# The order of all engine queues of a state-space convolution and feed-forward kernel, searched anew with altered planner costs

## Chip, cores and metric

One core of a Trainium2 chip. The metric is the time of one execution in microseconds, the median of several. The core's engines are TensorE (PE), VectorE (DVE), ScalarE (ACT), GpSimd (POOL) and SyncE (SP, which here issues DMAs); each runs its own queue of instructions in order and waits on semaphores.

## The reference

```python
x = A_q                                    # (1, 2048, 640), bf16
h = x + A_ref(layernorm(x), A_k, A_v, A_shift_k, A_ssm_k, A_ssm_D)
h2 = h + B_ref(layernorm(h), B_w_gate, B_w_up, B_w_down)

def A_ref(q, k, v, shift_k, ssm_k, ssm_D):
    k_shift = sum over t < 4 of k_pad[:, t:t + S, :] * shift_k[:, 3 - t]   # causal, per channel
    kv = k_shift * v
    y = irfft(rfft(kv padded to 2 S) * rfft(ssm_k padded to 2 S))[:S]       # causal long convolution, per channel
    return q * (y + kv * ssm_D)

def B_ref(x, w_gate, w_up, w_down):        # 640 -> 1728 -> 640
    return (silu(x @ w_gate) * (x @ w_up)) @ w_down
```

## The kernel before

The sequence is cut into four blocks of 512 rows. The long convolution is done block against block in a transformed domain: the four blocks of the filter are transposed and transformed (`ktrans`, `kfwd`, `kcomb`, tiles `KT`, `KO`, `C`, `R1`), each block of `kv` is formed (`kv`: short convolution on PE, transposed by DMA into `kvo`, times `v` on DVE) and transformed (`xfwd`: tiles `XH`, `FO`), products of block j of kv with block i - j of the filter are summed on DVE (`prod`, by far the most of DVE's work), and `inverse` gives rows again: DVE combines to `IE` and `IO`, PE multiplies with `itab`, ACT or DVE evicts, the gate with the normalized x and the second layer norm follow on ACT, DVE and POOL (which takes the power -1/2), and four DMA transposes put the block's normalized rows into `hnT`. `ffn` then does the up stage, thirteen PSUM tiles of ten matmuls (gate and up, 128 x 512 outputs) and one of five, each evicted twice by ACT (L964 with silu, L966) and multiplied on DVE (L968), and the down stage (L1000, L1012; for the last rows L983), added to x and stored. While PE does the feed-forward of block i, the other engines do the convolution of block i + 1.

The program is planned, not written in its final order. `g.add` records 921 tasks, numbered in order of recording, each with an engine, a planner's cost in nanoseconds and the data that it reads and writes. `ORDER` lists, for each engine, the numbers in the order in which its queue takes them. `schedule` walks the five queues with the costs, and from the modelled times it does two things only: it gives each PSUM tile one of four units (two banks each), the one that comes free first, and where PE would wait over 700 ns at the opening of a tile it puts `fill` idle matmuls of 192 columns (L250) before it. It also puts a wait behind a run of more than five independent DVE tasks. `emit` then writes the queues with their waits. `VECTOR` names the PSUM evictions that are done by DVE (L490 to L496) instead of ACT (L502).

What the numbers mean (block i's transform, say, is `xf` i):

| numbers | tasks |
|---|---|
| 0 to 4, 17 to 19, 57, 62, 67, 136 | first loads: identity, wcol, D row, ftab (3), itab (4), filter blocks (17, 57, 62, 67), kT of block 0 (18), v (19), x (136) |
| 13; 15, 16; 34 | warm-up matmuls; tables for the short convolution; adding D to the filter |
| 20 to 31 | kv of block 0: matmuls 20, 24, 28, evictions 21, 25, 29, PE transposes 22, 26, 30, products 23, 27, 31 |
| 32, 33, 35, 36; 58 to 61, 63 to 66, 68 to 71 | transposes of the filter (PE) and their evictions of 1280 columns |
| 37 to 56; 72 to 91; 94 to 113; 114 to 133 | filter transforms kf0 to kf3: PE task n, its eviction n + 1, then four DVE sums |
| 92, 93; 134, 135 | DVE combinations of filter blocks; the same by POOL's DMAs |
| 137 to 157; 327 to 342; 520 to 535; 727 to 741 | first layer norm of blocks 0 to 3 (338 a small DVE step of block 1, the last four each the normalized rows on ACT, L843) |
| 158 to 177; 343 to 362; 536 to 559; 750 to 769 | xf0 to xf3: PE task n, its eviction n + 1, then DVE sums |
| 182 to 221; 376 to 424; 583 to 631; 795 to 843 | inverse transform, gate and second layer norm: among them DVE's last combinations (188, 183; 383, 377, 384; 590, 591; 802, 796, 803), the powers on POOL (205, 212, ...), ACT steps ahead of them (204, 211, ...) and the hnT transposes (block 0: 200, 207, 214, 221; block 2: 604, 613, 622, 631; block 3: 816, 825, 834, 843) |
| 222 to 231 | loads of the feed-forward weights: GA, UA, GB, UB, PK, Wd |
| 232 on; 425 on; 632 on; 844 on | up stage of blocks 0 to 3: PE task n, gate eviction n + 1, up eviction n + 2, product n + 3 (the narrow tile has two of each) |
| 291 to 308; 484 to 501; 691 to 708; 903 to 919 | down stages, their evictions (487, 491, 496, 500 in block 1) and residual sums |
| 311, 504, 711; 312, 505, 712; 315 to 323, 508 to 516, 715 to 723 | loads of k and v of blocks 1 to 3, and the DMA transposes of the short convolution |

Of the kernel before, what the change touches and what calls it, by code (L numbers as in the profile page):

```python
# [58 lines left out]
class _Graph:  # L59
# [171 lines left out]
    def emit(self, block):  # L231
# [99 lines left out]
    """,  # L331
    "dve": """
# [10 lines left out]
    """,  # L343
    "pool": """
        8 10 6 11 5 9 7 151 202 216 195 205 209 219 198 212 134 336 135 403 421 394 412 529 610 619 628 601 736 822 813 840
        831
    """,
    "sp": """
# [4 lines left out]
}  # L353

VECTOR = """
    21 129
"""

def bass_sequential_preLN__ssm_conv_h3__swiglu_ffn__prompt_kernel(
# [38 lines left out]
    with ExitStack() as es:  # L398
# [54 lines left out]
        w = o + 16640  # L453
# [662 lines left out]
```

## Time and profile before

| | |
|---|---|
| runs | 268.63, 268.86, 268.97 us, median 268.86 |
| profiled execution | 268.22 us, of which the span is 266.3; granted TensorE clock 1.00 |
| PE | 254.0 us busy (95%), 1638 matmuls |
| DVE | 204.0 us (77%) |
| ACT | 203.9 us (77%) |
| POOL | 29.1 us (11%) |
| DMA | 28.47 MB moved in 43701 packets |
| matmuls of the up stages | 53.1 + 53.1 + 45.5 + 45.5 us by their modelled ends |

Busy times of PE overlap, since its matmuls are pipelined and their ends modelled (379 ns for one of 512 columns, where the next starts 0.22 us later). So idle time before an instruction tells more than busy time. Views that follow show instructions as start, duration, engine, line, operation, written and read tiles, with the idle time before it and its releaser in brackets.

### The profile page before, as it was taken

The page shows a single profiled execution, that of the slowest core. Times are in us where ns is not written, and L with a number is a line of the kernel's source. Part 1 is how long each engine was busy: PE and PEld are TensorE (multiplying, and loading weights), DVE is VectorE, ACT ScalarE, POOL GpSimd, SP SyncE. Part 2 cuts the span into 40 slices and gives each one's busy share as a digit, 9 for nine tenths or more (in the row PEclk, how much of TensorE's full clock was granted, in tenths as well). Part 3 has the DMA queues.
Part 4 walks back from the last instruction along what each step waited for, and adds up shares of the span by engine and source line. Part 5 has one row for each costly group of instructions (what it writes and reads, how often), then busy time and mean ns, then how long its engine had stood idle before and what let it go on. Part 6 is the DMA issues. An engine that isn't in the chain of part 4 may idle for free.

```text
span 266.3 us, 4177 instructions
## 1 busy us (share of the span) xinstructions
PE 254.0 (95%) x1638; PEld 142.1 (53%) x1638; DVE 204.0 (77%) x285; ACT 203.9 (77%) x392; POOL 29.1 (11%) x37
## 2 busy tenths in 40 slices
PE   7889888999999999999999999899999999999995
PEld 5567454545544646544445567444446674444563
DVE  0889999999999999999999999999895101330404
ACT  2689999999967999766979999678799982653600
POOL 0000314202030035000020041000300200000000
PEclk9999999999999999999999999999999999999999
DMA  6998919889966566331001734510000140000032
GB/s 155 335 333 266 342 57 227 131 194 315 178 111 108 81 173 105 55 117 81 4 0 19 184 79 93 146 78 1 2 0 0 22 79 0 0 2 0 0 127 74
DMA packets 43701, 28.47 MB, mean 107 GB/s; under 512 B 32289, under 2 KB 41378, under 8 KB 43682
## 3 DMA queue, kind: packets, MB, share of 16 engines
q1 hardware_dynamic: 41968, 25.58, 36.4%
q0 software_dynamic: 1056, 2.62, 5.7%
q8 instruction: 13, 0.21, 0.3%
q10 hardware_dynamic: 658, 0.01, 0.1%
q14 instruction: 6, 0.05, 0.1%
HBM read 15.69 MB, written 2.62 MB: 69 GB/s over the span
## 4 chain that ended last, share of the span: by engine, by line
PE 53%; ACT 23%; DVE 11%; DMA 6%; SPq 4%; issue 2%; POOL 0%; DVEq 0%
PE ps L941 16%; PE ps L942 15%; PE ps L1003 14%; SPq L514 3%; ACT xh L843 3%; ACT KT L502 3%; PE ps L610 2%; DMA kT<-in_A_k_dram 2%; ACT KO L502 2%; DMA ftab<-cst_ftab 2%; DMA hnT<-qo 2%; DVE gu L968 2%; PE ps L717 2%; ACT C L502 1%; ACT qo L884 1%
## 5 line engine op out<-in xcount | busy, mean ns | idle before, releaser
L1003 PE MATMUL ps<-Wd,gu 128*128 128x384 bf16 (+1 forms) x390 | 55.5, 299 | 0.1
L941 PE MATMUL ps<-hnT,GA 128*128 128x512 bf16 x140 | 53.1, 379 | 1.3 <-DMA hnT<-qo 1.1
L942 PE MATMUL ps<-hnT,UA 128*128 128x512 bf16 x140 | 53.1, 379 | 0.0
L1003 PEld LDWEIGHTS ps<-Wd,gu 128*128 128x128 bf16 x390 | 37.6, 98 | 17.1 <-issue 1.1
L941 PE MATMUL ps<-hnT,GB 128*128 128x512 bf16 x120 | 45.5, 379 | 0.0
L942 PE MATMUL ps<-hnT,UB 128*128 128x512 bf16 x120 | 45.5, 379 | 0.0
L966 ACT ACTIVATE ub<-ps 128x512 bf16<-128x512 f32 (+1 forms) x60 | 33.9, 567 | 14.9 <-PE ps L942 12.0
L964 ACT ACTIVATE gu<-ps 128x512 bf16<-128x512 f32 x52 | 30.4, 596 | 13.2 <-PE ps L942 13.1
L968 DVE TENSOR_TENSOR gu<-gu,ub 128x512 bf16<-128x512 bf16 x52 | 21.5, 421 | 23.8 <-ACT gu L964 15.8
L779 DVE TENSOR_TENSOR T<-X,C 128x2560 bf16<-128x2560 bf16 x20 | 29.7, 1486 | 0.2
L780 DVE TENSOR_TENSOR T<-X,C 128x2560 bf16<-128x2560 bf16 x20 | 29.7, 1486 | 0.1
L911 POOL TENSOR_TENSOR mv<-mv,half 128x1 f32<-128x1 f32 x16 | 16.1, 1010 | 69.1 <-ACT mv L904 69.1
L941 PEld LDWEIGHTS ps<-hnT,GA 128*128 128x128 bf16 x140 | 13.7, 98 | 18.4 <-DMA hnT<-qo 1.4
L610 PE MATMUL ps<-KT,ftab 128*128 128x320 bf16 x128 | 19.8, 300 | 3.5 <-ACT KT L502 1.1
L942 PEld LDWEIGHTS ps<-hnT,UA 128*128 128x128 bf16 x140 | 13.7, 98 | 15.6
L785 DVE TENSOR_TENSOR T<-T 128x1280 bf16<-128x1280 bf16 x24 | 19.5, 820 | 0.2
L941 PEld LDWEIGHTS ps<-hnT,GB 128*128 128x128 bf16 x120 | 11.7, 98 | 14.2 <-ACT gu L964 0.2
L942 PEld LDWEIGHTS ps<-hnT,UB 128*128 128x128 bf16 x120 | 11.8, 98 | 14.0
L831 POOL TENSOR_TENSOR st<-st,half 128x8 f32<-128x8 f32 x4 | 8.3, 2067 | 88.1 <-ACT st L825 88.1
L796 DVE TENSOR_TENSOR Y<-Y,T 128x2560 bf16<-128x2560 bf16 x12 | 17.8, 1484 | 0.0
L610 PEld LDWEIGHTS ps<-KT,ftab 128*128 128x128 bf16 x128 | 11.2, 98 | 10.9 <-ACT KT L502 2.0
L843 ACT ACTIVATE xh<-xh,st 128x640 bf16<-128x640 bf16 x16 | 14.7, 967 | 2.7 <-DVE st L833 2.7
(96 smaller groups left out, 381.9 us busy)
## 6 DMA issues: line engine op xcount, KB each, us to landing
kc<-in_A_ssm_k_dram SPq DMA_DIRECT2D x4, 640.0 KB, 9.4
xh<-in_A_q_dram SPq DMA_DIRECT2D x4, 640.0 KB, 4.1
vt<-in_A_v_dram SPq DMA_DIRECT2D x4, 640.0 KB, 4.5
out_dram<-xh SPq DMA_DIRECT2D x15, 160.0 KB, 1.9
Wd<-in_B_w_down_dram SPq DMA_DIRECT2D x1, 1280.0 KB, 6.3
C<-C POOLq DMA_DIRECT2D x1, 1280.0 KB, 9.6
C<-R POOLq DMA_DIRECT2D x1, 1280.0 KB, 9.4
UA<-in_B_w_up_dram SPq DMA_DIRECT2D x1, 1120.0 KB, 9.1
```

The lines of the kernel that those rows point to most:

```text
L610: last = e.matmul(pt.f(c, W), ftab[:, cs, j, f * P:(f + 1) * P], src[:, j, c * W:(c + 1) * W], start=(j == par), stop=(j == par + 2))
L779: g.add("dve", nm, lambda e, x=x, k=k, t1=t1: e.tensor_tensor(out=t1, in0=x, in1=k, op=ALU.mult), cdve(2560), r=[x, k], w=[t1])
L780: g.add("dve", nm, lambda e, x=x, k=ksw, t2=t2: e.tensor_tensor(out=t2, in0=x, in1=k, op=ALU.mult), cdve(2560), r=[x, k], w=[t2])
L785: g.add("dve", nm, lambda e, p=p, q=q, d=d, op=op: e.tensor_tensor(out=d, in0=p, in1=q, op=op), cdve(1280), r=[p, q], w=[d])
L796: g.add("dve", nm, lambda e, y=y, z=z: e.tensor_tensor(out=y, in0=y, in1=z, op=ALU.add), cdve(2560), r=[y, z], w=[y])
L843: g.add("act", nm, lambda e, j=j, xj=xj: e.activation(out=xj, in_=xj, func=ACTF.Identity, scale=s[:, 4, j:j + 1], bias=s[:, 5, j:j + 1]), ...
L941: e.matmul(pt.f(0, N), wg[:, c, f0:f0 + P], hnT[:, c, :], start=(c == 0), stop=(c == NC5 - 1))
L942: last = e.matmul(pt.f(1, N), wu[:, c, f0:f0 + P], hnT[:, c, :], start=(c == 0), stop=(c == NC5 - 1))
L964: g.add("act", nm, lambda e, pt=pt, gv=gv, a=ps_g, ts=ts: e.activation(out=gv, in_=pt.f(a[0], N, a[1])[:, ts], func=ACTF.Silu, scale=gain) ...
L966: g.add("act", nm, lambda e, pt=pt, uv=uv, a=ps_u, ts=ts: e.activation(out=uv, in_=pt.f(a[0], N, a[1])[:, ts], func=ACTF.Copy, scale=gain) ...
L968: g.add("dve", nm, lambda e, uv=uv, gv=gv: e.tensor_tensor(out=gv, in0=gv, in1=uv, op=ALU.mult), cdve(n), r=[gv, uv], w=[gv])
L1003: last = e.matmul(pt.flat(c1 - c0, P + c0), slots[fb][:, j * P:(j + 1) * P], Wd[:, fb, c0:c1], start=(fb == 0 and not second), stop=(fb == ...
```

## The change

Every queue's order is replaced, most tasks moving by a few places. `VECTOR` gives eviction 33 to DVE in place of 21, which goes to ACT. Four kinds of cost are altered: an ACT step that takes scale and bias per row from 186 to 219 ns above its base, the small ACT steps of the layer norms from 160 to 185, the evictions of the up stage at least 400 and its products at least 320. No task is added or taken out and no instruction is changed but for the engine of the two evictions. The diff, with the orders cut to the stretches that matter:

```diff
@@ -307,53 +307,53 @@
 
 ORDER = {
     "pe": """
-        13 32 35 20 24 28 22 41 43 37 47 51 26 39 49 45 30 65 160 162 164 158 172 168 170 166 58 63 60 80 68 84 76 86 78 70 82
-        72 74 114 98 94 191 193 190 192 118 126 128 116 120 108 317 321 124 104 102 106 313 100 96 122 236 232 240 248 343 345
-        347 349 244 256 355 351 357 264 353 252 260 268 276 272 280 284 386 388 387 385 291 506 292 510 293 514 297 301 302
-        536 306 540 550 538 542 548 425 546 544 429 445 437 433 453 449 441 461 457 469 477 465 473 593 595 594 484 592 485
-        717 486 713 494 495 721 490 499 750 762 754 758 764 756 752 760 636 632 640 648 644 668 652 660 656 664 676 680 672
-        684 805 807 804 691 806 692 693 701 702 706 697 868 856 848 864 844 852 860 876 884 872 888 880 892 896 903 904 905
+        13 32 35 20 24 28 22 41 43 37 39 26 51 47 49 30 45 65 164 160 162 158 60 58 166 170 172 63 168 94 80 70 82 86 76 74 72
+        84 98 78 68 191 193 190 192 126 128 120 118 313 321 116 100 104 114 106 96 108 317 102 122 124 232 236 240 244 343 347
+        345 349 252 351 260 355 357 268 353 256 248 272 276 264 280 284 386 388 387 385 291 506 292 510 293 514 297 301 302
+        536 306 548 540 550 542 546 425 544 538 429 445 437 433 441 453 449 461 469 457 465 477 473 593 595 594 592 484 721
+        713 485 717 486 494 495 490 499 762 764 760 754 756 750 752 758 644 636 632 640 660 652 648 656 668 684 664 672 676
+        680 805 807 804 691 806 692 693 701 697 702 706 864 848 852 844 856 868 860 880 872 888 876 896 884 892 903 904 905
         911 912 908 915 918
     """,
     "act": """
-        2 1 14 33 36 25 29 42 44 38 52 48 40 50 46 66 161 163 165 159 173 169 171 167 59 61 150 81 69 77 64 85 79 71 155 73 87
-        75 115 99 83 157 154 156 95 203 217 204 218 196 119 197 210 121 117 211 127 318 109 125 322 105 103 107 101 314 123 97
...
-        463 459 470 458 471 478 467 479 466 535 475 474 533 482 605 623 614 481 607 534 608 625 596 626 718 532 714 616 609
-        598 487 617 618 611 627 496 722 620 599 612 621 629 600 630 602 603 491 500 751 763 755 759 765 757 761 753 633 637
-        727 634 728 642 641 649 729 645 730 638 731 669 650 732 733 653 646 734 654 661 735 662 657 658 738 670 665 741 666
-        677 739 681 678 673 740 674 685 686 817 689 688 835 682 819 808 820 810 821 837 811 823 812 838 826 824 814 828 839
+        1 2 14 36 21 29 25 42 44 38 40 52 48 50 46 66 161 163 159 165 61 59 171 167 150 64 173 169 95 81 71 87 83 75 77 73 85
+        99 155 79 156 154 157 69 203 204 217 127 196 218 197 210 119 121 211 322 117 101 105 115 107 97 314 109 103 318 125
+        123 327 328 233 237 234 329 330 238 242 241 245 344 246 348 346 350 331 332 352 253 254 333 261 334 358 356 262 335
...
+        528 470 451 459 471 458 533 466 479 478 467 532 475 474 482 605 623 614 535 534 596 607 608 481 722 625 714 598 609
+        718 626 599 600 616 611 617 618 602 627 612 603 496 487 491 620 621 629 630 500 763 761 765 755 757 751 753 645 759
...
+        727 633 638 637 728 634 729 641 730 661 646 642 731 654 732 733 649 650 734 735 653 662 657 685 669 658 741 670 665
+        739 666 673 740 674 677 678 738 681 686 689 817 682 819 688 820 808 821 835 810 837 826 823 811 838 812 824 828 814
...
     """,
     "dve": """
-        12 16 15 34 21 137 138 139 140 141 142 143 23 144 27 145 146 31 147 53 55 54 56 148 174 149 175 178 179 176 181 180
-        177 152 185 184 187 186 153 188 182 189 183 201 90 215 194 208 88 129 206 89 220 91 199 92 213 93 130 363 364 365 366
...
-        337 255 379 378 381 376 380 267 382 263 383 275 271 377 338 279 384 399 283 560 417 562 287 561 390 290 408 563 564
...
-        578 579 580 581 440 582 436 559 583 448 585 586 444 588 587 456 589 530 452 590 531 464 743 460 472 742 468 480 584
-        591 745 744 606 746 476 748 624 770 483 747 772 749 615 597 771 775 773 726 774 488 776 725 777 724 778 780 497 492
-        779 501 781 782 766 783 785 784 787 786 635 788 767 789 643 768 790 791 639 792 651 769 647 793 655 797 663 794 737
-        798 799 659 800 671 801 795 802 667 679 796 803 687 818 675 690 809 836 683 827 699 704 851 695 859 847 867 708 855
-        863 871 879 875 887 883 891 899 895 902 906 909 916 913 919
+        12 15 33 16 137 138 139 140 34 141 142 143 23 27 53 31 144 145 55 146 147 54 148 56 149 174 175 179 178 181 180 176
+        152 177 182 185 184 187 186 153 188 189 90 183 201 215 194 208 88 206 129 91 220 89 199 93 213 92 130 363 131 112 364
...
+        337 378 379 251 381 380 271 338 376 259 382 267 383 275 384 279 377 560 399 417 562 408 283 564 287 561 290 563 566
...
+        558 578 579 436 580 440 581 585 582 587 448 444 586 456 742 464 583 588 452 589 530 472 460 590 531 743 480 468 584
+        591 745 744 606 747 746 597 476 748 624 749 483 770 771 615 772 773 775 774 777 726 776 725 724 492 778 497 779 501
+        488 780 781 782 783 785 766 784 787 768 767 786 639 635 788 769 789 647 791 643 790 793 792 651 655 794 663 797 737
+        659 799 798 671 800 667 801 795 802 679 803 796 675 818 687 809 683 836 690 827 695 851 847 859 855 699 867 708 704
+        863 875 883 871 891 879 887 899 902 895 913 906 909 916 919
     """,
     "pool": """
-        8 10 6 11 5 9 7 151 202 216 195 205 209 219 198 212 134 336 135 403 421 394 412 529 610 619 628 601 736 822 813 840
+        8 9 6 10 11 5 7 151 202 216 195 205 209 219 198 212 134 336 135 421 412 403 394 529 610 601 619 628 736 822 813 840
         831
     """,
     "sp": """
-        17 0 18 136 3 19 62 226 67 57 310 227 230 223 225 4 222 311 312 207 221 200 214 224 320 315 316 323 319 228 229 504
-        231 505 509 508 513 512 516 406 397 424 415 305 300 309 296 503 711 712 720 715 716 719 723 613 622 604 631 489 498
-        493 502 710 825 816 843 834 907 709 700 705 696 917 910 914 920
+        17 0 18 136 3 19 62 57 227 4 67 222 310 224 312 223 311 225 207 221 200 214 316 315 226 320 323 230 319 228 231 505
+        229 504 509 508 513 516 512 424 406 397 415 305 309 300 296 503 711 712 716 719 720 723 715 604 613 622 631 498 493
+        489 502 710 825 816 843 834 700 914 696 910 907 705 709 917 920
     """,
 }
 
 VECTOR = """
-    21 129
+    33 129
 """
...
@@ -473,7 +473,7 @@
-            return 60 + 0.833 * n + 93 * ptr
+            return 60 + 0.833 * n + (93 * ptr if ptr < 2 else 219)
@@ -822,7 +822,7 @@
-                g.add("act", nm, lambda e: e.activation(out=s[:, 2, :], in_=s[:, 1, :], func=ACTF.Identity, bias=epc[:, 0:1]), 160,
+                g.add("act", nm, lambda e: e.activation(out=s[:, 2, :], in_=s[:, 1, :], func=ACTF.Identity, bias=epc[:, 0:1]), 185,
@@ -901,7 +901,7 @@
-                    g.add("act", nm, lambda e, m=m, ep=ep: e.activation(out=m[:, 2:3], in_=m[:, 1:2], func=ACTF.Identity, bias=ep), 160,
+                    g.add("act", nm, lambda e, m=m, ep=ep: e.activation(out=m[:, 2:3], in_=m[:, 1:2], func=ACTF.Identity, bias=ep), 185,
@@ -911,7 +911,7 @@
-                    g.add("act", nm, lambda e, m=m: e.activation(out=m[:, 4:5], in_=m[:, 0:1], func=ACTF.Identity, scale=m[:, 3:4]), 160,
+                    g.add("act", nm, lambda e, m=m: e.activation(out=m[:, 4:5], in_=m[:, 0:1], func=ACTF.Identity, scale=m[:, 3:4]), 185,
@@ -962,11 +962,11 @@
-                          cact(n), w=[gv], pr=[pt])
+                          max(400, cact(n)), w=[gv], pr=[pt])
-                          cact(n), w=[uv], pr=[pt])
+                          max(400, cact(n)), w=[uv], pr=[pt])
-                          cdve(n), r=[gv, uv], w=[gv])
+                          max(320, cdve(n)), r=[gv, uv], w=[gv])
```

15 rows, old and new, of the table ORDER are left out of this document.

## The prediction

> **What bounds the kernel now.** I read the busy shares by stretch first, cut where the work changes: the start, the transform of the filter with block 0's up stage (FFN up: gate and up matmuls), block 1, the passage from block 1 to 2, block 2's up stage, the passage to block 3, and the end.
>
> ```profile
> core 0: us, PE busy (x) PEld busy (x) DVE busy (x) ACT busy (x) POOL busy (x), PEclk, DMA share, GB/s
> 15.30:48.00 32.70, 28.17 (x245) 18.54 (x243) 32.16 (x48) 31.98 (x53) 6.83 (x9) 1.00 0.78 235
> 48.00:87.00 39.00, 39.00 (x217) 19.51 (x216) 38.40 (x50) 33.90 (x65) 4.69 (x4) 1.00 0.80 172
> 87.00:141.00 54.00, 52.85 (x323) 27.73 (x322) 53.41 (x71) 45.01 (x96) 7.82 (x5) 1.00 0.35 76
> 141.00:170.00 29.00, 27.84 (x217) 17.77 (x215) 28.64 (x37) 28.63 (x56) 4.36 (x4) 1.00 0.46 106
> 170.00:201.00 31.00, 30.95 (x149) 14.27 (x150) 30.16 (x38) 23.73 (x49) 2.62 (x1) 1.00 0.10 31
> 220.00:262.00 42.00, 42.00 (x232) 21.77 (x231) 9.47 (x21) 15.57 (x31) 0.00 (x0) 1.00 0.06 20
> ```
>
> Three engines are full in turn, at full clock throughout. DVE is busy 182.8 of the 185.7 us from 15.3 to 201. ACT is full in the first stretch and in 141 to 170. PE is full from 48 on except for about a microsecond each in 87 to 141 and 141 to 170, and after 220 it alone sets the time. So a reordering can only win what PE loses after 48 (and the ends), and only as far as ACT and DVE follow. Two of PE's waits that come after the start, from the list of waits (total, times, longest):
>
> ```profile
> PE ps L941 <- DMA hnT<-qo: 1.1, 1, 1.1
> PE ps L717 <- DMA kT<-in_A_k_dram: 0.6, 1, 0.6
> ```
>
> The largest of these waits lies at 170, on the way from block 1 to 2. The chain that ended last goes through it:
>
> ```profile
> 164.43 0.69 ACT dn L1023
> 165.11 0.54 SPq L514
> 165.69 4.31 DMA hnT<-qo
> 170.05 0.39 PE ps L941
> ```
>
> The last of four transposes of block 2's normalized rows was issued at 165.69 and took 4.31 us; PE had finished its other work at 165.80 + 3.15 = 168.95:
>
> ```profile
> 165.80 3.15 PE L610 MATMUL ps<-vt,ftab 128*128 128x320 bf16 x22
> DMA to landing us min/median/max: 2.6/2.8/4.4
> q8 instruction: 1, 0.02, 2.5%
> ```
>
> The second line is the landing time of all sixteen such transposes, so this one is about 1.5 us late against the median. The third is the instruction queue in the DMA view of 167.0 to 169.5: one packet of 0.02 MB held one of 16 engines for 2.5% of 16 x 2.5 us = 1.0 us, just when that transpose was in flight. I take the excess to be this: PE's own program being fetched through an engine that still had a piece of the transpose to do.
>
> **The change, part by part.** The tasks and their dependencies stay (one eviction and another change engines); what moves is their order, by a few places.
>
> *Start, to 20 us.* Eviction 33 goes from ACT to DVE and 21 the other way, the products for kv0 come before the D row, so the first kv0 matmuls can go some half a microsecond sooner. It brings nothing:
>
> ```profile
> 7.19 5.14 DMA ftab<-cst_ftab
> 12.37 2.90 PE ps L610 x20
> 15.28 1.24 DVE vt L736
> 20.42 0.59 ACT X L502
> ```
>
> The transform table lands at 12.3 whatever was done before, and its issue keeps its place as the fifth on SP; the product at 15.28 waits for v, the sixth, also unmoved. PE now does tile 39 before 26 instead of waiting for that product, so ACT reaches the end of the kt2 eviction up to 0.5 us sooner; but ACT's next, 161, needs PE's 160, which now stands second behind 164 (0.54 us of matmuls), and the products 27, 53, 31 ahead of them on DVE run back to back as before. Both come to 20.3. Term: 0 (-0.2 to +0.3).
>
> *ACT from 20.3 to 52.5.* Before the first up tile stand the same 62 PE tasks and, on ACT, the same 64 but for three evictions left behind it, worth the same (one of 1024 columns and two of 640). ACT had no gap here but 0.2 us. Term 0; bounds -0.2 and +0.5, the latter if the evictions, whose order no longer follows PE's so closely (95 81 71 87 against PE's 94 80 70 82 86), find a PSUM tile unfinished once.
>
> *Block 1, 48 to 141.* Here DVE decides, since PE reaches the inverse transform as DVE finishes its input. The work on DVE ahead of it is the same; what can go are idle times.
>
> ```profile
> 46.58 1.54 POOL L911 TENSOR_TENSOR mv<-mv,half 128x1 f32<-128x1 f32 x1 [1.31 <-ACT mv L904]
> 48.15 0.45 DVE L919 TENSOR_SCALAR qo<-xh,mv 128x640 bf16<-128x640 bf16 x1 [0.44 <-POOL mv L911]
> 59.71 0.96 DVE L748 TENSOR_TENSOR vt<-vt,kvo 128x1536 bf16<-128x1536 bf16 x1 [0.17 <-DVE vt L748]
> 88.61 3.61 SPq L514 DMA_TRANSPOSE kT<-in_A_k_dram  x1
> 94.37 0.41 PE L717 MATMUL ps<-kT,dg 64*64 64x512 bf16 x4 [0.61 <-DMA kT<-in_A_k_dram]
> ```
>
> ACT's step 211 ahead of that power moves up one place and the tile's transposes 316, 315 are issued first: of 0.44 + 0.17 us I take half, 0.3. The first pair's input (383) now has 271 and 338 ahead of it, which PE's second pair makes up. The load of k for block 2 is issued when the second matmul group of the inverse is done, so 0.3 passes on to 94.37 and the following up stage. Term: -0.3 (-0.6 to +0.3). The row of the 1.54 us power shows it ending 0.4 us after a product of 1.49 us that began at 46.22. [...]
>
> *Passage to block 2, 141 to 170.* ACT's list up to the last normalized row has one task more, the down eviction 491:
>
> ```profile
> 161.64 0.29 ACT L914 ACTIVATE mv<-mv 128x1 f32<-128x1 f32 x1
> 161.83 0.29 ACT L904 ACTIVATE mv<-mv,epc 128x1 f32<-128x1 f32 x1
> 163.18 0.29 ACT L914 ACTIVATE mv<-mv 128x1 f32<-128x1 f32 x1 [0.25 <-POOL mv L911]
> 163.50 0.92 ACT L916 ACTIVATE qo<-xh,mv 128x640 bf16<-128x640 bf16 x1
> 168.02 1.33 ACT L502 ACTIVATE FO<-ps 128x640 bf16<-128x640 f32 x2
> 7.33 0.82 PE L250 MATMUL ps<-ident 128*128 128x192 bf16 x8
> 25.41 0.66 PE L250 MATMUL ps<-ident 128*128 128x192 bf16 x6
> ```
>
> A step that depends on the one just before it starts 0.03 us after that (163.18 + 0.29 to 163.50), an independent one 0.10 us before its end (161.64 + 0.29 to 161.83). The new list has five such pairs here where two stood, 3 x 0.13 = 0.4 us more. The wait of 0.25 for the power may go or double. The last transpose, so far at 165.69, is then issued at 165.1 to 165.8, since the 0.69 us eviction that stood after the last row only changes places with it. The two waits that were filled with 8 and 6 idle matmuls (last two rows) fall in the part of the start that the new order tightens, so up to 14 of them go, each with its weight load. By that many instructions the fetch moves back in the rest of the program: 14 matmuls at 3.15 us / 22, about 2 us of work, past the landing. Then the up stage starts when ACT has freed a tile, the fifth of eight evictions, the first of the 168.02 row: about 168.02 + 1.33/2 = 168.7, plus 0.4, less the 0.3 from above and something for the wait: 169.0 instead of 170.05. Term: -1.1 counted from the start, so -0.8 more (-1.2 to 0, the zero if the fetch still strikes).
>
> *Passage to block 3.*
>
> ```profile
> 187.30 0.42 DVE L968 TENSOR_TENSOR gu<-gu,ub 128x512 bf16<-128x512 bf16 x1 [0.63 <-ACT ub L966]
> 199.21 2.34 PE L860 MATMUL ps<-IO,itab 128*128 128x320 bf16 x16
> 199.49 1.55 DVE L581 TENSOR_TENSOR IE<-Y 128x1280 bf16<-128x1280 bf16 x2
> 201.05 0.79 ACT L884 ACTIVATE qo<-ps,st 128x640 bf16<-128x640 f32 x1
> 201.90 0.85 PE L860 MATMUL ps<-IE,itab 128*128 128x320 bf16 x5 [0.35 <-ACT qo L884]
> ```
>
> PE needs DVE's last input (ready at 199.49 + 1.55 = 201.04) and a PSUM tile freed by ACT at 201.84. DVE must therefore come 0.3 us sooner for a gain of 1.1: it has the 0.3 from block 1 and the 0.63 us at 187.30, which was a wait for the late up stage; the product 667, put ahead of the first pair, takes back 0.42. ACT's list just ahead of that tile is as long as before: one normalized row (738 for 740), one up or gate eviction and two short ones. Term +0.1 (-0.4 to +0.5). The remaining 60 us are PE's down and up matmuls, unchanged.
>
> *End.*
>
> ```profile
> 263.64 0.47 DVE L992 SCALAR_TENSOR_TENSOR xh<-ps,st,xh 128x256 bf16<-128x256 f32 x1
> 259.88 3.69 PE L985 MATMUL ps<-Wd,gu 128*128 128x384 bf16 x26
> ```
>
> Residual 913 leaves its place before the last one, which could start at 259.88 + 3.69 = 263.57 instead of 263.64; the store order matters little. Term: -0.05 (-0.2 to +0.1). The four altered costs act through the planner alone (tile choice and number of filling matmuls).
>
> Sum: 0 + 0 - 0.3 - 0.8 + 0.1 - 0.05 = -1.05, say -1.0 us. The profiled execution took 268.22 us (266.3 span and 1.9 around it) and would take 267.2; the median of the runs shown, 268.86, lies 0.64 above it, so I say 267.9. Differences below 0.2%, 0.54 us, can't be told from none.
>
> **Rivals.** *The transpose is late again.* The fetch, or the stores behind it, strike the transpose as before. For it: the transpose itself moves by tenths only, and the fetch may not move at all if the number of filling matmuls stays. Then 0.8 is gone: -0.2, 268.6, no change. [...] *The change does nothing* (all gaps are taken up elsewhere) gives the old 268.9.
>
> *VectorE becomes the bound, slower.* Its queue is in order. Gate-up products (271, 452, 460 with 472, 667) now stand earlier, and each waits if ACT's eviction isn't done, with all convolution work queued behind. The price of one is the row at 187.30: 0.63. Three are 1.9; less the 0.3 gained, the last input comes at 201.04 + 1.6 = 202.6 and PE starts at 202.7 instead of 201.90: +0.8, 269.7. It decides once the new waits exceed 201.84 - 201.04 + 0.3 = 1.1 us. Against it: on DVE's 185 us only one such wait stood before.
>
> **How the numbers follow.** Forecast 0.55; late transpose 0.19; nothing 0.06; VectorE bound 0.20. The forecast's own terms add to -2.5 at best and +1.2 at worst, which don't fall together: its range is 266.7 to 268.3. With the rivals, 266.6 to 269.6 leaves out 2 in 10. Faster by over 0.2%: 0.55; within it: 0.25; slower: 0.20.
>
> **What would show it.** Right: the wait of PE for hnT gone and the first up matmul of block 2 near 169.0; the last hnT transpose at 2.6 to 2.8 us; no instruction packet in its flight; DVE without the 0.63 us before a gate-up product; the first up matmul of block 0 still at 52.5; the last four PE groups unchanged. Wrong: DVE waits for ACT over 1 us in sum before 201, ACT gaps before 52, or a PE wait at the start of block 3's up stage near 219, where the old trace had none.

## The result and the profile after

The changed kernel takes 270.27 us (median of nine runs, 269.49 to 272.02), the kernel before 268.83 on the same chip: a ratio of 1.0071 (95% interval 1.0048 to 1.0094). It is slower; 267.9 was forecast. The nine runs form two groups by the granted clock of TensorE: five at 1.0 (269.49 to 270.27) and four at 0.994 (271.63 to 272.02), whose medians lie 1.8 us apart. The profiled execution, 271.95 us with a span of 270.1, is of the second group, so its account is told with and without the clock's part. In this text kT1 is the DMA transpose of k for block 1 (kT2 and kT3 those for blocks 2 and 3), kv1 the matmuls that read it (313, 317, 321), kvt1 the transposes of the result, and kf the filter transforms. From the page after, the size and the clock's row, and the filling matmuls from the view of their line:

```profile
span 270.1 us, 4214 instructions
PE 256.0 (95%) x1650; PEld 144.4 (53%) x1667; DVE 202.7 (75%) x285; ACT 205.8 (76%) x392; POOL 27.6 (10%) x37
PEclk9999998899999999999999999999999999999999
```

```profile
L250 PE MATMUL ps<-ident x43: 246/246/257, 7.5 to 42.6; 128*128 128x192 bf16 x43
```

There are 43 filling matmuls where 14 stood: 6 ahead of task 20, 12 ahead of 94, 19 ahead of 191, 6 ahead of 313. With their weight loads TensorE's program is 58 instructions longer from block 1 on. The forecast had up to 14 of them go.

TensorE's waits after, from the list of waits, are to be read against the 1.1 us for hnT and 0.6 us for kT of before:

```profile
PE ps L717 <- DMA kT<-in_A_k_dram: 3.2, 3, 2.2
PE ps L712 <- DMA kT<-in_A_k_dram: 1.7, 1, 1.7
```

The wait for hnT is gone. In its place TensorE waits 4.9 us for transposed k, 2.2 of it in block 1 and 1.7 in block 3. These two places, from the timeline of PE:

```profile
42.23 0.66 PE L250 MATMUL ps<-ident 128*128 128x192 bf16 x6
45.10 1.41 PE L717 MATMUL ps<-kT,dg 64*64 64x512 bf16 x16 [2.22 <-DMA kT<-in_A_k_dram]
46.85 1.49 PE L712 MATMUL ps<-kT,dl 128*128 128x512 bf16 x3 [0.33 <-DVE C L692]
48.13 4.48 PE L610 MATMUL ps<-KT,ftab 128*128 128x320 bf16 x28
...
154.62 0.81 PE L712 MATMUL ps<-kT,dl 128*128 128x512 bf16 x3 [1.70 <-DMA kT<-in_A_k_dram]
```

and ScalarE at the first of them, whose next eviction needs what TensorE could not yet make:

```profile
44.84 0.29 ACT L904 ACTIVATE mv<-mv,epc 128x1 f32<-128x1 f32 x1
48.38 0.60 ACT L502 ACTIVATE kT<-ps 128x512 bf16<-128x512 f32 x1 [3.24 <-PE ps L712]
```

Before, kv1 waited for ScalarE and not for kT1, and ScalarE had no gap there:

```profile
45.78 1.06 PE L717 MATMUL ps<-kT,dg 64*64 64x512 bf16 x16 [0.82 <-ACT KO L502]
46.77 1.04 PE L712 MATMUL ps<-kT,dl 128*128 128x512 bf16 x4
46.94 1.07 ACT L502 ACTIVATE kT<-ps 128x1024 bf16<-128x1024 f32 x1
```

ScalarE's gap of 3.24 us opens as kT1 lands: its next task in order, 322, needs kv1's matmuls, and these run at half clock. Sixteen 64-row matmuls take 1.41 us where they took 1.06. In the busy shares by stretch (stretch and length, then the engines' busy times) the granted clock is the third number from the end, 0.50 in the slow part:

```profile
42.40:45.00 2.60, 0.48 (x6) 0.26 (x4) 2.57 (x5) 2.60 (x9) 1.39 (x2) 1.00 1.11 352
46.00:47.00 1.00, 0.67 (x9) 0.28 (x3) 0.69 (x1) 0.00 (x0) 1.00 (x1) 0.50 1.78 58
48.00:49.00 1.00, 1.00 (x5) 0.52 (x4) 1.00 (x1) 0.60 (x1) 0.00 (x0) 0.50 1.04 219
49.00:50.00 1.00, 1.00 (x9) 0.71 (x8) 0.10 (x1) 0.65 (x2) 0.00 (x0) 0.96 0.69 131
```

Both late transposes, kT1 and kT3, took longer from issue to landing. That time is the last number of these lines, from the DMA views of 37 to 48 and 142 to 156 us, first of before, then of after:

```profile
kT<-in_A_k_dram SPq DMA_TRANSPOSE x1, 5.6
...
kT<-in_A_k_dram SPq DMA_TRANSPOSE x1, 5.0
```

```profile
kT<-in_A_k_dram SPq DMA_TRANSPOSE x1, 7.0
...
kT<-in_A_k_dram SPq DMA_TRANSPOSE x1, 6.3
```

The trace of before has 3311 instructions of TensorE and 13 packets of 16 KB on the instruction queue q8, one for 255 instructions. These packets, by that count, are taken here for the blocks of TensorE's program. In the records of single packets after, such a block starts at 43.1 us and kT1 lands at 45.06; another starts at 152.2 and kT3 lands at 154.35. Before, the blocks near there start at 47.3 and 150.6, after the landings at 44.64 and 149.19.

The way between fixed points shows where the time went. The points: ScalarE's 161, the first up matmul of blocks 0, 1 and 2, the first kv matmul of block 2 (506), the end of the last down group (918). Rows are worked out from the tasks' own records in each trace, in us. In the rows after, kf first, 19 fewer fills and kvt1 first, 17 matmul records are missing, that of a stage's first matmul mostly among them, so that these entries are good to about 0.15:

```
                          161 at  to up 0  to 506  to up 1  to up 2  to 918
before                     20.32   32.22   41.83    17.80    57.88   93.52
after                      19.39   35.97   42.56    18.23    58.12   93.23
after, kf first            19.24   32.83   41.85    18.81    58.43   93.24
after, 19 fewer fills      19.37   32.95   41.43    19.09    56.85   93.24
after, kvt1 first          19.14   36.00   41.38    18.91    58.26   93.23
after, 24 more fills       19.09   34.36   42.42    18.23    57.01   93.39
after, 52 instr. in ff1    19.40   35.98   43.06    18.73    56.72   93.39
after, both                19.35   32.42   43.08    17.79    56.64   93.38
after, both + kvt1         19.71   32.44   42.08    17.74    56.62   93.39
before, 27 instr. early    20.33   32.20   41.80    17.80    56.86   93.52
before, 39 instr. early    20.25   32.22   41.57    17.84    56.79   93.53
before, 29 instr. later    19.62   32.25   41.89    17.80    56.72   93.52
```

From before to after: -0.93 at the start, +3.75 to block 0's up stage, +0.73, +0.43, +0.24, -0.29, and -0.19 for the last stores, together the 3.74 us between the two spans. Of the loss, 2.8 us lie ahead of block 0's up stage; behind it the stretches gain and lose tenths.

### The profile page after: what moved, and what is told of

It is laid out like the page before. It is cut to its first block, busy times and chain, and to the rows that moved or that the text cites. A ratio compares the mean times of both kernels' runs of the same rounds, so it can differ in the third digit from the quotient of the medians.

```text
span 270.1 us, 4214 instructions
## 1 busy us (share of the span) xinstructions
PE 256.0 (95%) x1650; PEld 144.4 (53%) x1667; DVE 202.7 (75%) x285; ACT 205.8 (76%) x392; POOL 27.6 (10%) x37
## 4 chain that ended last, share of the span: by engine, by line
PE 65%; DVE 11%; ACT 9%; DMA 9%; SPq 3%; issue 1%; DVEq 0%
PE ps L942 19%; PE ps L941 18%; PE ps L1003 15%; DMA kT<-in_A_k_dram 4%; PE ps L610 4%; PE ps L860 3%; DMA kvo<-kT 2%; SPq L514 2%; ACT C L502 2%; DMA ftab<-cst_ftab 2%; PE ps L952 2%; DVE T L779 2%; DVE Y L785 1%; ACT kT L502 1%; PE ps L985 1%
## 5 line engine op out<-in xcount | busy, mean ns | idle before, releaser
L941 PE MATMUL ps<-hnT,GA 128*128 128x512 bf16 x131 | 49.6, 379 | 0.0
L941 PE MATMUL ps<-hnT,GB 128*128 128x512 bf16 x117 | 44.3, 379 | 0.1
L941 PEld LDWEIGHTS ps<-hnT,GA 128*128 128x128 bf16 x140 | 13.7, 98 | 17.2 <-issue 0.5
L942 PEld LDWEIGHTS ps<-hnT,UA 128*128 128x128 bf16 x140 | 13.7, 98 | 15.8
L911 POOL TENSOR_TENSOR mv<-mv,half 128x1 f32<-128x1 f32 x16 | 14.3, 901 | 67.3 <-ACT mv L904 67.3
L1030 DVE TENSOR_TENSOR xh<-xh,dn 128x640 bf16<-128x640 bf16 x12 | 5.7, 485 | 17.4 <-ACT dn L1023 17.4
```

The costliest lines, as they stand in the source:

```text
L911: g.add("pool", nm, lambda e, m=m: e.tensor_tensor(out=m[:, 3:4], in0=m[:, 2:3], in1=half[:, 1, 0:1], op=ALU.pow), 650, r=[m[:, 2:3], half ...
L941: e.matmul(pt.f(0, N), wg[:, c, f0:f0 + P], hnT[:, c, :], start=(c == 0), stop=(c == NC5 - 1))
L942: last = e.matmul(pt.f(1, N), wu[:, c, f0:f0 + P], hnT[:, c, :], start=(c == 0), stop=(c == NC5 - 1))
```

## The experiments

Two theories: **O**, the order draws block 1's kv matmuls ahead of the work that covered the wait for kT1; **F**, the longer program moves the blocks in which TensorE's instructions are fetched onto the transposes kT1 and kT3. Two smaller ones: **C**, the half clock is a cost of its own; **S**, two loads on SP's queue hold up the transposes kvt1. "Called for" is an estimate from the trace of before: its packets at 191.85 and 235.54 us start when 2456 and 2968 instructions of TensorE have started, 512 apart and both 152 past a multiple of 256, and every block is reckoned as called for at that count. The eleven other packets of that trace start 0.5 to 4.7 us behind the moment so reckoned.

**One cause at a time, in the changed kernel.** The order alone:

```diff
-  pe:  ... 118 313 321 116 100 104 114 106 96 108 317 ...
+  pe:  ... 118 116 114 108 313 321 100 104 106 96 317 ...
-  act: ... 322 117 101 105 115 107 97 314 109 103 318 ...
+  act: ... 117 115 109 322 101 105 107 97 314 103 318 ...
```

> The changed kernel, with one edit: three groups of kf matmuls (116, 114, 108) stand again ahead of block 1's kv matmuls (313, 321) on TensorE, and their evictions (117, 115, 109) ahead of 322 on ScalarE, as in the kernel before. The filling matmuls ahead of 313 go with it. Theory O (order: kv1's matmuls were drawn ahead of the work that covered the wait for kT1): TensorE's stall at 42.6 us falls from 2.4 to about 0.8 us, ScalarE's idle time ahead of 322 from 3.24 to about 1.0 us, the granted clock is 1.00 in every run, the first up matmul of block 0 starts near 53.0 instead of 55.35, and the time is 268.9 to 269.4 (the changed kernel's runs at full clock had 270.0). Theory F (fetch: TensorE's instruction blocks now land on the transposes kT1 and kT3): kT1 still lands at 45.0 and kT3 still takes 6.3 us; the work that is drawn ahead is only missing later, and the full-clock time stays within 0.3 of 270.0.

268.57 us, 0.3 below what O expected; ratio to before 1.0004 (0.9990 to 1.0019), clock 0.999 or 1.00 in all twelve runs.

```profile
45.30 1.06 PE L717 MATMUL ps<-kT,dg 64*64 64x512 bf16 x16 [0.31 <-DMA kT<-in_A_k_dram]
```

```profile
47.37 0.60 ACT L502 ACTIVATE kT<-ps 128x512 bf16<-128x512 f32 x1 [0.60 <-PE ps L712]
```

kT1 still takes 7.3 us and kv1 starts no earlier (45.30), but ScalarE waits 0.60 instead of 3.24 and block 0's up stage starts at 52.06. O holds for that place; F's claim that the covering work would only be missing later fell. kT3 stayed late (6.6 us). The instruction block alone:

```diff
         g.schedule(ORDER)
+        for s, n in {94: 0, 191: 12}.items():
+            g.tasks[s].fill = n
```

> The changed kernel, with 19 filling matmuls less (none instead of 12 ahead of task 94, 12 instead of 19 ahead of 191), so that TensorE's program is 38 instructions shorter from there on; the order is untouched. Theory F: the instruction block that came while kT1 was being issued (38.0 to 40.8 us) is called for about 2.5 us later, behind its issue, so kT1 takes 5.6 instead of 7.0 us from issue to landing, and kT3 5.0 instead of 6.3; TensorE's stall at 42.6 falls to about 1.0 and that at 152.6 to below 0.5; the clock stays at 1.00; the time is 267.5 to 268.7. Theory O: kT1's and kT3's times from issue to landing are those of the changed kernel within 0.3 us, and the time stays at 270.0 or above.

267.27 us, 0.9953 (0.9932 to 0.9974). In the changed order, untouched, both transposes take their old time, and TensorE's wait at kv1 is 0.82:

```profile
kT<-in_A_k_dram SPq DMA_TRANSPOSE x1, 5.6
...
kT<-in_A_k_dram SPq DMA_TRANSPOSE x1, 5.0
```

```profile
43.70 1.06 PE L717 MATMUL ps<-kT,dg 64*64 64x512 bf16 x16 [0.82 <-DMA kT<-in_A_k_dram]
```

So most of the loss needs both: with either edit alone the time is no longer above that of before. Together, with the filling matmuls down to 14:

```diff
-  pe:  ... 118 313 321 116 100 104 114 106 96 108 317 ...
+  pe:  ... 118 116 114 108 313 321 100 104 106 96 317 ...
...
+        for s, n in {94: 0, 191: 8}.items():
+            g.tasks[s].fill = n
```

> The changed kernel with both edits: kf ahead of kv1 (order) and 29 filling matmuls less than the changed kernel (14 remain, as before the change; none ahead of 94, 8 ahead of 191, none ahead of 313). If O and F are two causes that add, TensorE's stall at 42.6 us is gone, the first up matmul of block 0 starts near 51.5 (52.1 with the order alone, 52.3 with the fills alone), kT3 lands in 5.0 us, block 2's up stage starts near 169.0, and the time is 266.4 to 267.1. If each of them alone already removes the same wait, the time is that of the fewer fills, 267.0 to 267.6.

267.22 us, 0.9931 (0.9906 to 0.9957): the second half of the expectation, by which each edit alone removes the same wait. Block 0's up stage did come sooner (51.77), but the way from there to 506 took 43.08 instead of 41.43; 0.9 of that is kT2, which took 6.1 us in this profile instead of 5.2.

**The half clock.**

```diff
+        for s, n in {313: 30}.items():
+            g.tasks[s].fill = n
```

> The changed kernel with 30 instead of 6 filling matmuls ahead of 313, so that TensorE works until kT1 lands. The fetch of kT1's time was called for before them and stays: kT1 still takes 7.0 us, and 313 still starts near 45.1. Theory C (the half clock after the stall of 2.4 us is a cost of its own): the granted clock is 1.00 in every run, kv1's and kf's matmuls after 313 take their usual time, the first up matmul of block 0 starts at 53.4 to 53.8 instead of 55.35, and no run lies above 270.6. kT3's block moves by 48 instructions as well, ahead of kT3's issue, which gives up to 1.4 us more: 268.3 to 268.9 in all. Without C, ScalarE's evictions set that start anyway and it stays at 55.2 or later.

269.23 us, 1.0020 (1.0004 to 1.0036), clock 1.00 in all twelve runs, none above 269.78. kT1 takes 7.2 us as before this edit, and 313 starts at its old time, at full clock:

```profile
44.99 1.06 PE L717 MATMUL ps<-kT,dg 64*64 64x512 bf16 x16 [0.41 <-DMA kT<-in_A_k_dram]
45.98 1.04 PE L712 MATMUL ps<-kT,dl 128*128 128x512 bf16 x4
53.45 0.39 PE L941 MATMUL ps<-hnT,GA 128*128 128x512 bf16 x1
```

ScalarE's gap is still 2.22 us, the part of the late kT1. The way to the first up matmul, the last row, shrinks from 35.97 to 34.36: the half clock costs about 1.6 us, near the 1.8 between the two groups of runs. The total missed its expectation by 0.3; a block now fell among kvt1's transposes (one took 4.0 us), and the way from there to 506 stayed at 42.4.

**The same block, in the kernel before.** Waits that are long fulfilled lengthen TensorE's program, with no work and no other order:

```diff
+            if t.seq in (160, 162, ...):
+                for _ in range(3):
+                    prog["pe"].append(lambda e, h=sems["act"], v=kn["act"]: e.wait_ge(h, v))
```

> The kernel before, with waits that are long fulfilled ahead of fifteen groups of TensorE between 19 and 29 us: 27 instructions more, no work and no other order. Theory F puts the instruction block that was called for at 42.6 us, behind kT1's issue (39.0 to 41.8 us), into that issue: kT1 takes about 7.1 instead of 5.6 us from issue to landing, and TensorE's wait ahead of block 1's kv matmuls grows from 1.0 to about 2.4 us. From there on all later blocks come about 1.9 us earlier too: the one at 165.3 us comes at 163.4, in a transpose that is not the last, so that block 2's up stage starts a good 1.0 us sooner after its predecessor, as in the twin run with the same instructions placed later. So this run is to be read against that twin: 0.5 to 1.5 us slower than it (ScalarE had no idle time there, and gets about 1.0). The rival, that kT1's 7 us in the changed kernel came from the weights issued beside it (UB behind it, GA ahead of it): kT1 stays at 5.6 here, and both twins have the same time.

267.58 us, 0.9945 (0.9927 to 0.9963). The first half missed: kT1 stayed at 5.6, since the block, called for at 40.9, came only at 45.8, behind kT1. So this run could not decide between F and its rival, the traffic beside kT1. Its twin has the waits behind kT1:

```diff
-            if t.seq in (160, 162, ...):
+            if t.seq in (232, 240, 248, ...):
```

> The kernel before, with the same kind of waits ahead of fifteen groups of TensorE between 54 and 75 us: 29 instructions more behind kT1. Theory F: kT1 stays at 5.6 us; block 2's last hnT transpose lands in 2.6 instead of 4.3 us and its up stage starts without the 1.25 us stall; block 3's first transpose (4.4 us) is at 2.6, which nothing waits for; time 267.4 to 268.0 against 268.8. [...]

267.36 us, 0.9928 (0.9908 to 0.9949). The way from block 1's up stage to block 2's takes 56.7 us instead of 57.9. So the profiles show 1.2 us of the 1.7 at that place; their starts differ by another 0.7, and the start varies from run to run. With six groups more in the early list:

```diff
-            if t.seq in (160, 162, ..., 86):
+            if t.seq in (160, 162, ..., 86, 78, 70, 82, 72, 98, 94):
```

> The kernel before with 39 instead of 27 instructions of fulfilled waits between 19 and 37 us. With 27 the block was called for near the end of kT1's issue and came behind it (45.8 us; kT1 5.6 us). With 39 it is called for at about 40.0 us, 1.0 us after the issue began, as in the changed kernel. Theory F: kT1 takes 7.0 to 7.3 us instead of 5.6, TensorE waits for it until about 46.0 instead of 44.7, ScalarE gets about 1 us of idle time ahead of kv1's first eviction, and the first up matmul of block 0 starts 0.5 to 1.4 us later than with 27; the time is 268.0 to 269.0 against 267.6 with 27. The rival (the block only seems to be the cause; kT1's time belongs to the new order's traffic): kT1 5.6 and 267.4 to 267.8.

267.49 us, 0.9965 (0.9943 to 0.9988). Now the block starts at 43.1 and kT1 takes 6.5 instead of 5.6: in the old order, with its old traffic, the block alone makes kT1 late, though less than the 7.0 that F expected. And it costs nothing; the time is the one that the rival had (the line numbers lie three further down in this program):

```profile
45.71 1.06 PE L720 MATMUL ps<-kT,dg 64*64 64x512 bf16 x16 [0.81 <-ACT KO L505]
```

In the order of before, TensorE's wait ahead of kv1 is for ScalarE to free a PSUM tile; kT1, landing at 45.48, isn't last. That answers what was left between O and F. On the way to block 0's up stage the late kT1 costs 0.0 in the old order (32.22 against 32.20), 0.4 with kf first (32.83 against 32.42), and about 1.4 in the changed order (34.36 against 32.95), where the half clock that follows from it adds about 1.6. The order alone, with kT1 in time, costs about 0.7 (32.95 against 32.22); together these are the 3.75 us. Each of these figures compares single profiles.

**The passage to block 2.** Twenty instructions of such waits in block 1's up stage, in the kernel before:

```diff
+            if t.seq in (437, 433, 453, 449, 441, 461, 457, 469, 477, 465):
...
```

> The kernel before, with two waits more that are long fulfilled ahead of each of ten groups of block 1's up stage on TensorE: 20 instructions more, between 117 and 142 us, no work and no other order. Theory F: the instruction block that came while hnT's last transpose of block 2 was being issued (165.7 to 167.0 us) is called for about 1.2 us earlier, before that issue, so this transpose lands 2.6 instead of 4.3 us after its issue, TensorE's stall of 1.25 us at 168.7 goes, block 2's up stage starts near 169.0 instead of 170.05, and the time is 267.7 to 268.1 against 268.8. The rival: the late landing belongs to the transposes of that place or to the traffic beside it, the landing stays at 4.3 us, and the time is 268.8 or up to 0.5 above, for the waits.

268.12 us, 0.9980 (0.9962 to 0.9997), just outside what was expected. The block moved, but onto hnT's third transpose (4.3 us), behind which the last took 3.5; the stall shrank from 1.09 to 0.51. In the changed kernel, 26 and then 52 instructions, by three and then seven waits ahead of each group:

```diff
+            if t.seq in (425, 429, 445, ..., 477):
+                for _ in range(3):
...
```

> The changed kernel with 26 instructions of fulfilled waits in block 1's up stage (118 to 145 us): the block that is called for at 149.8 us, in kT3's issue (148.1 to 150.8), comes ahead of it; all before 118 us is untouched, the half clock too. Theory F: kT3 5.0 instead of 6.3 us, TensorE's stall of 1.76 us at 152.6 falls to 0.4, and the time is 1.1 to 1.5 lower in each state of the clock (268.5 to 268.9 at full clock). The rival: hnT of block 2 and ScalarE's evictions were next in line, and less than 0.5 of it arrives at block 2's up stage.

271.80 us, 1.0121 (1.0097 to 1.0145): a miss. The block was called for as kT3's issue began, and kT3 took 6.2. Five of six runs had the half clock.

```diff
-                for _ in range(3):
+                for _ in range(7):
```

> The changed kernel with 52 instead of 26 instructions of fulfilled waits in block 1's up stage. With 26 the block was called for at 147.8 to 148.4 us, just as kT3's issue began (147.9), and kT3 still took 6.2 us. With 52 it is called for near 145.5, over 2 us ahead of that issue. Theory F: kT3 4.8 to 5.2 us, TensorE's stall of 1.6 to 1.8 us there falls below 0.6, the way from block 1's first up matmul to block 2's takes 56.7 to 57.3 us instead of the 58.0 with 26 waits and the 58.1 without, and the time is 0.8 to 1.4 us below that with 26 waits in each state of the clock (271.0 at half clock, 269.2 at full clock). If kT3 lands early and that way still takes 57.7 or more, hnT of block 2 or the evictions were next in line.

269.18 us, 1.0037 (1.0014 to 1.0061), three of twelve runs at half clock. kT3 is free, and the passage takes 56.72 us:

```profile
kT<-in_A_k_dram SPq DMA_TRANSPOSE x1, 4.9
```

The late kT3 thus cost 1.4 us (58.12 to 56.72), and nothing stood next in line.

**SP's queue, the durations, and all together.**

```diff
-  sp:  ... 316 315 226 320 323 230 319 228 ...
+  sp:  ... 316 315 320 323 319 226 230 228 ...
```

> The changed kernel, with one edit: on SP's queue the loads 226 and 230 stand behind the five transposes of kvt1 instead of between them. Theory S (these two loads hold up the transposes for which VectorE's 324 and TensorE's 343 wait): the last of the five lands near 62.2 instead of 63.5, VectorE's idle time of 1.17 us ahead of 324 and TensorE's stalls of 0.68 and 0.35 us near 64 and 66.6 go, and the time is 0.6 to 1.0 lower in each state of the clock (269.0 to 269.4 at full clock). The rival: what TensorE gains there, it waits for later in block 0's up stage, and the time stays within 0.3 of 270.0 at full clock.

270.18 us, 1.0055 (1.0033 to 1.0077); by the clock, 269.3 (median of six at 1.0) and 270.6 (six at 0.994), against 270.0 and 271.8. That is 0.6 lower at full clock, the least that S expected. But in this profile VectorE's wait ahead of 324 fell only from 1.17 to 0.84, since a block struck the last of the five transposes (4.0 us), and most of what the way to 506 gained is kT2, 4.75 us instead of 5.68. The mechanism of S shows in the last version below. The four durations, alone in the order of before:

```diff
-            return 60 + 0.833 * n + 93 * ptr
+            return 60 + 0.833 * n + (93 * ptr if ptr < 2 else 219)
...
-                          cdve(n), r=[gv, uv], w=[gv])
+                          max(320, cdve(n)), r=[gv, uv], w=[gv])
```

> The kernel before, in its own order, with the four durations alone. The number of filling matmuls ahead of each task comes out as it was (8 and 6), and nothing else depends on them but which of two waits of an instruction comes first. All theories: 268.8 within 0.4; if it differs by more, the durations do something to the program that was overlooked.

268.74 us, 1.0007 (0.9989 to 1.0024): nothing. The last version has the order of kf first, the 14 filling matmuls, the SP edit, and 16 instructions of waits in block 1's up stage:

```diff
+            if t.seq in (433, 441, 453, 449, 461, 469, 457, 465):
+                for _ in range(3):
...
```

> As the run with both edits, and besides the two loads behind kvt1's transposes on SP's queue and 16 fulfilled waits on TensorE in block 1's up stage, so that the instruction block of 165 us does not come in hnT's last transpose of block 2. Theories S and F: 0.3 to 0.8 lower than with both edits alone, 266.0 to 266.6. The rival: block 1's and block 2's passages are bound by VectorE and ScalarE by now, and the time is that of both edits within 0.3.

266.45 us, 0.9896 (0.9873 to 0.9919), the fastest here: 0.77 below both edits alone. Here S holds: VectorE's wait of 0.98 and TensorE's of 0.43 for kvt1's last transpose, which the run with both edits still has, are gone, and the way to 506 takes 42.08 instead of 43.08 at equal kT2 (6.2 and 6.1 us). Against the old order with its 29 waits, on the same chip, it is 0.9 lower.

## Why the prediction was wrong

*What bounds the kernel* held: what was won or lost is what TensorE lost, and ahead of 52 us, what ScalarE lost.

*Start, 0*: it came 0.93 sooner in the profile. Over all traces 161 starts at 19.1 to 19.7 in the changed program and at 19.0 to 20.7 in the old one, with the landing of v (13.6 to 14.3; 13.7 to 15.6). Why v lands late more often there was not tried.

*ACT from 20.3 to 52.5, 0 (-0.2 to +0.5)*: this step failed, by 3.75 us. The count of the tasks ahead of the first up tile was right, and their sum is unchanged; what it leaves out is which of them stand around an event that does not move. 116, 114 and 108, which stood ahead of kv1, now stand behind it, so kT1's landing, which had slack, became the last thing waited for. By the experiments about 0.7 of the 3.75 us is this order alone, about 1.4 the kT1 that an instruction block made late, and about 1.6 the half clock.

*The filling matmuls, "up to 14 of them go"*: the sign was wrong, 29 came. The planner's rule that sets their number stood in the code and could have been worked through; the trace of the old order cannot show it. With them the forecast's own reading, a block on a transpose in flight, turned against it at kT1 and kT3 (7.0 and 6.3 us where they took 5.6 and 5.0).

*Block 1, -0.3*: nothing in any run. The wait of 0.44 us for POOL's power stood in the profile after as before:

```profile
47.13 0.45 DVE L919 TENSOR_SCALAR qo<-xh,mv 128x640 bf16<-128x640 bf16 x1 [0.44 <-POOL mv L911]
```

To 506 and on to block 1's up stage took 59.6 before, 60.8 after, and 59.8 at best in the changed order. In the profile after, a block fell on one of kvt2's transposes (4.1 us; VectorE then sat idle for 1.18), and the way from 506 on took 0.4 longer.

*Passage to block 2, -0.8 (-1.2 to 0)*: the size of the delay and its tie to the block were right, the way to its end was not. The passage shrinks from 57.88 to between 56.6 and 57.0 us in each profile of the table in which kT3 and hnT's last transpose came in time, in the old order too, so it is the block's place that gives this and not the new order. In the change itself the block did not move back, as forecast, but forward, onto the first two of hnT's four transposes (4.2 and 3.5 us). The last took 2.6, and TensorE's wait for it is gone: that was luck. The late kT3 took the gain back: +0.24. The terms of tenths in this step were not tested singly. The rival "late again" had named the fetch, but only for the same transpose. With a block in flight beside it a transpose took 0.9 to 1.7 us longer: kT1 6.5 to 7.3 instead of 5.6, kT3 6.3 instead of 5.0, hnT's last of block 2 4.3 in the profile before instead of 2.6 in the one after.

*Passage to block 3, +0.1, and end, -0.05*: -0.29 to the end of 918 and -0.19 behind it; the 0.63 us gap of VectorE went, as said.

*VectorE as the bound, slower*: the sign came true, the mechanism didn't. Ahead of 200 us no gate-up product waited over 0.3 us; VectorE's long gap (2.77 us at 49.1) waited for evictions held up by ScalarE's 3.24.

The first up matmul of block 0, named at 52.5 as the sign that ScalarE's step holds, stood at about 55.3.

*The range*: the bounds of the six terms add to -2.8 and +1.7, not to -2.5 and +1.2. With +1.7 a range of the terms would have reached 270.6 and held the measured time, but for none of the reasons that the terms give.

## What to carry to other kernels

When an order is changed by a few places, list for each transfer what stands ahead of its first user in both orders, not only the sum of work up to a later point: kT1's landing, with 1.1 us of slack before (44.64, and kv1 at 45.78), became the bound when three tasks changed sides. Work out everything the planner derives from the order, here the number of idle matmuls, since instructions that do no work still moved the blocks in which the program is loaded: the one that started at 47.3 us before came at 45.8 with 27 waits ahead of it and at 43.1 with 39. Where a transpose is late without cause, shift the program by some twenty to fifty harmless instructions before reordering anything: 29 of them gave 0.7% here. The number has to be found by trial: 26 in the changed kernel gave nothing.

## What the runs showed of the hardware

kT1 and kT3 landed later where an instruction block was fetched while they were in flight. In 15 traces, kT1 took 6.5 to 7.3 us in the seven in which a block's packet started at 42.8 to 43.2 us, and 5.6 to 5.7 in the eight in which it started at 45.4 or later, behind the landing. With the order untouched it went both ways: 39 waits in the kernel before took kT1 from 5.6 to 6.5 us, 19 fewer filling matmuls in the changed kernel from 7.0 to 5.6. The 16 KB packet itself takes about 1 us (0.88 to 1.44 in the traces of before and after); the landing comes some 2 us after its start (in the profile after 2.0 for kT1, 2.2 for kT3). The moment of the block went with it too: kT3 took 6.2 to 6.6 us where a block started 2.6 to 4.3 us after kT3's issue began, but 4.9 and 5.2 us where it started 0.5 and 0.7 us after (52 waits; 24 more fills), and 4.8 to 5.0 without one. That the delay comes of a DMA engine that both share, as the prediction took it, no run shows.

The granted clock halved after a short gap, in some runs only. TensorE's stall for kT1, 2.2 to 2.4 us in the profiles of the four programs that had it (2.22 in the changed kernel, 2.25 with kvt1 first, 2.18 and 2.39 with 26 and 52 waits), brought a clock of 0.50 for 3.4 us, which set in 0.2 to 1.2 us after the stall had ended (from 45.7 to 49.1 us in the profile after). By their mean clock of 0.993 or 0.994, which is what one such stretch makes (1.7 us lost of 270), 18 of the 39 runs of these programs had it; stalls of up to 2.0 us (2.01 for kT3 with kf first, all twelve runs at 0.999 or 1.00) never showed it. Why the other 21 went without it was not shown.
